# Turning the experts' rows on VectorE: 32x32 squares that the loads bring to their partitions

## The chip, the cores and the metric

The kernel runs on one core of a Trainium2 chip. The metric is the device time of one execution in microseconds; a smaller one is better. Before the change it is 262.52 us, the median of three runs (262.42 to 263.04). TensorE multiplies matrices, VectorE (DVE in the profile), ScalarE (ACT) and GpSimd (POOL) work on elements, SyncE (SP) issues most of the transfers between HBM and the on-chip memory.

## The reference, cut to what matters

Two blocks follow each other. The first is a state-space scan over chunks (Mamba2): for 4 sequences with 8 heads of 768 steps it gives rows of 32 numbers. The heads of a step are put side by side, so that there are 3072 tokens of 256 numbers. The second block sends each token to one of 8 experts:

```python
x = attn_out.transpose(0, 2, 1, 3).reshape(B * S, H * D)      # 3072 x 256
logits = x @ w_gate                                            # 3072 x 8
expert_idx = np.argmax(logits, axis=1)
probs = softmax(logits)                                        # + 1e-09 in the sum
gate_w = probs[np.arange(N), expert_idx]
for e in range(8):
    xe = x[expert_idx == e]
    h = np.maximum(xe @ w1[e], 0.0)                            # 256 -> 1024
    out[expert_idx == e] = gate_w[...] * (h @ w2[e])           # 1024 -> 256
```

Everything is in fp32.

## The kernel before, in words

**Scan and routing, up to about 70 us.** Twelve steps (`d` from 0 to 11) compute the scan for 256 tokens each. `rows(d)` turns a step's result on TensorE into one row per token, and its constant matrix `turn` appends the terms of the logits; `rows_out(d)` multiplies by a decay on VectorE and stores the row in the tile `rt`. A row has 320 words in two halves of 160 (128 words of the token, then 32 terms of the logits), and one word more for the token's number (`TOK`), 321 words or 1284 bytes. `logits_of`, `choose`, `rank` and `ranked` find each token's expert and its place there. `place(k)` has GpSimd scatter 128 rows to the tensor `x_hbm` in HBM, which has a stretch of rows for each expert. `cut` and the extra place rules see to it that the first 256 rows of experts 0 and 1 are there before the last groups are placed. `empty_rest` writes empty rows behind each expert's last token.

**Experts, from about 70 us on.** There are 16 jobs: pass 0 takes the first 256 places of each expert (`P1`), pass 1 up to 192 further ones (`P2`), two experts at a time, where the two half tiles of 64 rows share one tile of 128 partitions (`xh`). For a job `m_load(i)` brings the rows from `x_hbm` with the token on the partitions, by DMAs on SyncE's queue. For a matmul the token's words have to be on the partitions. `m_xT(i, pp)` does that: TensorE transposes each tile of 128x128 (L519) into a PSUM bank, VectorE copies it to `xT` (L521, L525, L527), and `gates` computes the softmax weight from the row's terms of the logits: on VectorE a sum (L358), a maximum and a difference, on ScalarE an exponential (L492), on VectorE a sum and a reciprocal. `m_h(i)` computes the first layer in 8 slices `f` (L557), each followed by a relu on ScalarE into `hT` (L566); `m_y(i)` the second layer (L592), whose result is scaled by the gate (L577, L579) and scattered by GpSimd to the output under the token's number (L570).

What sets the order: the engines' streams are written out by hand (`tc.manual_schedule()`), and each engine runs its own in that order. In pass 0 `m_xT(i + 1)` stands inside `m_h(i)`, between slices 4 and 5, and so does the exponential in ScalarE's stream. For i = 1 the checks of `over()` stand there too, ahead of it. In pass 1 `m_xT(i + 2)` stands between the first layers of a pair and their second layers. The DMA queue of SyncE is served in its order: after job 1's load the load of job 2, the 8 pieces of expert 2's weights, the load of job 3, and so on. A load of `x_hbm` waits for the scatters that stand before it in the program, and a scatter to `x_hbm` waits for the loads that stand before it. Job 0 has a version of its own (`m_xT0`), whose result ScalarE copies (L507).

Of the kernel before, what the change touches and what calls it, by code (L numbers as in the profile page):

```python
# [46 lines left out]
def ssd_then_moe(ctx, tc, xs_in, ae_in, wgx, w_gate, w1, w2, gx, gb, gc, ga, out):  # L47
# [416 lines left out]
    def m_load(i):  # L464
        p, e = jobs[i]
        if p == 0:
            xs = mo.tile([128, 2, W], FP32, name="xs", bufs=7)
            nc.sync.dma_start(out=xs, in_=x_hbm[e * NR:e * NR + P1, :].rearrange("(t p) w -> p t w", p=128))
            ex[i]["xs"] = [xs[:, t] for t in range(2)]
            ex[i]["all"] = xs  # L470
            return
        xs = mo.tile([128, 2, W], FP32, name="xs", bufs=7)
        nc.sync.dma_start(out=xs[:, 0], in_=x_hbm[e * NR + P1:e * NR + P1 + 128, :])
        ex[i]["xs"] = [xs[:, 0]]
        ex[i]["all"] = xs
        if e % 2 == 0:
            xh = mo.tile([128, W], FP32, name="xh", bufs=2)
            for u in range(2):
                r0 = (e + u) * NR + P1 + 128
                nc.sync.dma_start(out=xh[64 * u:64 * u + 64, :], in_=x_hbm[r0:r0 + 64, :])  # L480
            ex[i]["xh"] = ex[i + 1]["xh"] = xh

    def gates(rows, n):
# [3 lines left out]
        logits(l, rows)  # L487
# [12 lines left out]
    def m_xT0():  # L500

        ex[0]["xT"] = mo.tile([128, KT, P1], FP32, name="xT", bufs=4)
        for k in range(KT):
            q = h_next()[:, 0:P1]
            for t, xs in enumerate(ex[0]["xs"]):
                nc.tensor.transpose(q[:, 128 * t:128 * t + 128], xs[:, 160 * k:160 * k + 128], ident)
            nc.scalar.copy(ex[0]["xT"][:, k], q)  # L507

    def m_xT(i, pp):
        p, e = jobs[i]  # L510
        for u in range(1 + p):
            ex[i + u]["xT"] = mo.tile([128, KT, P1], FP32, name="xT", bufs=4)
        tiles = [xs for u in range(1 + p) for xs in ex[i + u]["xs"]] + ([ex[i]["xh"]] if p else [])
        q = []
        for t, xs in enumerate(tiles):
            if t % 2 == 0:
                q.append(h_next().rearrange("p (t k m) -> p t k m", t=2, k=KT))
            for k in range(KT):
                nc.tensor.transpose(q[-1][:, t % 2, k], xs[:, 160 * k:160 * k + 128], ident)  # L519
        if p == 0:  # L520
            nc.vector.tensor_copy(ex[i]["xT"].rearrange("p k (t m) -> p t k m", t=2), q[0])  # L521
            ex[i]["g"] = gates(ex[i]["all"], 2)
            return
        for u in range(2):
            nc.vector.tensor_copy(ex[i + u]["xT"][:, :, 0:128], q[0][:, u])  # L525
# [455 lines left out]
```

## Time and profile before

| | before |
|---|---|
| median of 3 runs | 262.52 us (262.42 to 263.04) |
| the profiled execution | 261.87 us |
| its span in the trace | 260.2 us |
| TensorE busy | 246.1 us (95%) |
| VectorE, ScalarE, GpSimd busy | 88.5, 88.3, 84.3 us |
| granted TensorE clock, mean over the span | 0.989 |
| DMA | 39.29 MB, mean 151 GB/s |

The times of the profile come from one execution; 1.67 us of it lie outside the span. An engine's busy time is the sum over its instructions; neighbouring matmuls overlap, so what one of them costs in the stream is read from the starts of it and of the next, not from its duration. The granted clock is the share of TensorE's full clock that the chip allowed. The share of DMA is the mean over 16 DMA engines; where packets overlap it can pass 1. The word behind an arrow in a row is what ended the wait ahead of the instruction.

### The profile page before, as it was taken

How to read it: one execution, taken by the hardware profiler on the slowest of the kernel's cores; microseconds unless marked ns; L12 is line 12 of the kernel's file. 1: busy time of each engine (PE TensorE's matmuls, PEld its weight loads, DVE VectorE, ACT ScalarE, POOL GpSimd, SP SyncE). 2: the span in 40 equal slices, each digit the busy share in tenths (PEclk: the TensorE clock that was granted, in tenths of full speed). 3: DMA queues.
4: the chain of work that ended last, by engine and by line, in shares of the span. 5: the costliest groups of instructions: out<-in, count | busy, mean ns of one | idle time of the engine just before them, and what ended most of it. 6: DMA issues, size and time to landing. Idle time of an engine off the chain costs nothing. (4 is left out here: it accounts for less than half of the span.)

```text
span 260.2 us, 5524 instructions
## 1 busy us (share of the span) xinstructions
PE 246.1 (95%) x2072; PEld 207.8 (80%) x2072; DVE 88.5 (34%) x286; ACT 88.3 (34%) x291; POOL 84.3 (32%) x149
## 2 busy tenths in 40 slices
PE   8898899979699999999999999999999999999992
PEld 5576677656588888888888888888998968989781
DVE  5899687667522130202020201106125015052000
ACT  4575557530141323232231313232250520623300
POOL 3645768862635133341331111110311111113031
PEclk9999999997999999999999999999999999999998
DMA  6999878326323996967969601010103101201001
GB/s 195 309 370 332 290 228 289 142 78 207 135 78 91 337 403 207 334 215 256 279 221 319 212 25 45 0 40 4 44 5 83 37 4 44 73 5 39 3 15 43
DMA packets 21049, 39.29 MB, mean 151 GB/s; under 512 B 3004, under 2 KB 8446, under 8 KB 20992
## 3 DMA queue, kind: packets, MB, share of 16 engines
q1 hardware_dynamic: 18000, 30.12, 35.3%
q0 software_dynamic: 2880, 8.41, 8.7%
q8 instruction: 29, 0.48, 0.8%
q14 instruction: 28, 0.23, 0.3%
q10 hardware_dynamic: 112, 0.05, 0.1%
HBM read 29.51 MB, written 9.59 MB: 150 GB/s over the span
## 5 line engine op out<-in xcount | busy, mean ns | idle before, releaser
L557 PE MATMUL h_ps<-xT,w 128*128 128x256 f32 (+3 forms) x512 | 90.7, 334 | 0.3 <-ACT xT L507 0.2
L557 PEld LDWEIGHTS h_ps<-xT,w 128*128 128x128 f32 x512 | 80.2, 190 | 7.3 <-ACT xT L507 0.5
L592 PE MATMUL y_ps<-w,hT 128*128 128x256 f32 x384 | 85.2, 380 | 0.2 <-ACT hT L566 0.2
L592 PEld LDWEIGHTS y_ps<-w,hT 128*128 128x128 f32 x384 | 72.5, 190 | 10.6 <-ACT hT L566 0.6
L570 POOL DMA_INDIRECT out_dram<-yo,xs x24 | 23.8, 990 | 94.1 <-ACT yo L579 55.1
L277 DVE TENSOR_TENSOR M<-g,mask 128x1024 f32<-128x1024 f32 x24 | 28.2, 1216 | 8.4 <-PE g L272 5.7
L566 ACT ACTIVATE hT<-h_ps 128x256 f32<-128x256 f32 x64 | 23.3, 381 | 20.7 <-PE h_ps L557 15.9
L408 POOL DMA_INDIRECT x_hbm<-rows,pos x24 | 23.8, 993 | 15.1 <-DVE less L426 5.9
L521 DVE COPY xT<-h_ps 128x512 f32<-128x512 f32 x7 | 4.8, 692 | 64.1 <-PE h_ps L519 34.8
L632 ACT ACTIVATE hT<-h_ps 128x128 f32<-128x128 f32 (+2 forms) x64 | 18.3, 292 | 24.1 <-PE h_ps L557 23.3
L342 PEld LDWEIGHTS r<-turn,yT 128*128 128x128 f32 x96 | 14.0, 197 | 8.2 <-issue 4.3
L579 ACT ACTIVATE yo<-y_ps,t_gt 128x256 f32<-128x256 f32 x14 | 6.6, 474 | 40.5 <-PE y_ps L592 40.5
L342 PE MATMUL r<-turn,yT 128*128 128x160 f32 x96 | 16.9, 320 | 3.7 <-issue 3.0
L329 PE MATMUL y<-M,xp 128*32 128x128 f32 x384 | 15.1, 277 | 3.6 <-DVE M L277 2.7
L335 ACT COPY yT<-y 128x512 f32<-128x512 f32 (+1 forms) x13 | 7.1, 554 | 29.4 <-PE y L329 17.9
L525 DVE COPY xT<-h_ps 128x256 f32<-128x256 f32 x8 | 3.0, 419 | 39.1 <-PE h_ps L519 39.1
L265 POOL TENSOR_TENSOR xp<-xs_n,Ei 128x256 f32<-128x256 f32 x23 | 13.8, 620 | 5.5 <-DVE last L240 3.3
L329 PEld LDWEIGHTS y<-M,xp 128*32 128x32 f32 x384 | 10.3, 109 | 6.6 <-issue 4.3
L260 ACT ACTIVATE cm<-xs_n,par 128x128 f32<-128x128 f32 x46 | 15.1, 419 | 1.2 <-DMA xs_n<-in_xs_dram 1.2
L492 ACT ACTIVATE t_sub<-t_sub 128x8 f32<-128x8 f32 (+1 forms) x20 | 4.2, 211 | 32.9 <-DVE t_sub L491 31.4
L272 PE MATMUL g<-cm,xs_n 32*128 32x256 f32 x192 | 15.1, 431 | 0.0
L570 POOL DMA_INDIRECT out_dram<-yh,xh x4 | 3.9, 984 | 34.2 <-ACT yh L606 21.9
(126 smaller groups left out, 167.0 us busy)
## 6 DMA issues: line engine op xcount, KB each, us to landing
w<-in_w_dram SPq DMA_DIRECT2D x64, 256.0 KB
xs_n<-in_xs_dram SPq DMA_DIRECT2D x20, 320.0 KB
xs<-x_hbm SPq DMA_DIRECT2D x8, 321.0 KB
xs<-x_hbm SPq DMA_DIRECT2D x8, 160.5 KB
xs_n<-in_xs_dram SPq DMA_DIRECT2D x4, 192.0 KB
x_hbm<-zrows SPq DMA_DIRECT2D x1, 642.0 KB
xh<-x_hbm SPq DMA_DIRECT2D x8, 80.2 KB
xs_n<-in_xs_dram SPq DMA_DIRECT2D x4, 128.0 KB
```

The lines of the kernel that those rows point to most:

```text
L260: nc.scalar.mul(t[:, u], st[n]["CT"], par[:, u:u + 1])
L265: eng.tensor_tensor(out=t, in0=st[n]["x"].rearrange("p (h d) -> p h d", d=D), in1=bc(Ei[:, n, :, None], [128, NH, D]), op=ALU.mult)
L272: nc.tensor.matmul(g_ps[:, q, n % 2], lhsT=st[n]["BT"][r], rhs=st[n]["cm"][r].rearrange("p u i -> p (u i)"), start=True, stop=True)
L277: nc.vector.tensor_tensor(out=t, in0=g_ps[:, :, n % 2].rearrange("p q (u i) -> p q u i", u=2), in1=bc(mask[:, None, None, :], [128, 4, 2, ...
L329: nc.tensor.matmul(y_ps[o:o + D, h // 4, CH * s:CH * s + CH], lhsT=st[n]["xp"][:, D * h:D * h + D], rhs=st[n]["M"][:, h], start=first, sto ...
L342: nc.tensor.matmul(r_ps[:, s, 160 * t:160 * t + 160], lhsT=sd[d]["yT"][:, t, CH * s:CH * s + CH], rhs=turn[:, t].rearrange("p e h -> p (e ...
L408: s_ = nc.gpsimd.indirect_dma_start(out=x_hbm[:, :], out_offset=bass.IndirectOffsetOnAxis(ap=at, axis=0), in_=row, in_offset=None)
L557: nc.tensor.matmul(p[:, 0:n], lhsT=w[:, c:c + 128], rhs=xT[:, t, 0:n], start=(t == 0), stop=(t == KT - 1))
L566: nc.scalar.activation(ex[i]["hT"][:, f, 0:n], q, func=ACT.Relu)
L570: return nc.gpsimd.indirect_dma_start(out=out[:, :], out_offset=bass.IndirectOffsetOnAxis(ap=tok, axis=0), in_=yo[:, :], in_offset=None, b ...
L592: nc.tensor.matmul(p, lhsT=ex[i]["hT"][:, f, 128 * t:128 * t + 128], rhs=w_sb[e][1][:, f * DM:f * DM + DM], start=(f == 0), stop=(f == FT ...
L632: nc.scalar.activation(ex[i + u]["hT"][:, f, 0:n], q, func=ACT.Relu)
```

## The change

The rows in HBM get another order: the 256 words of the token first, in one piece, then the 64 terms of the logits, then the token's number sixteen times, 336 words or 1344 bytes. `rows_out` writes the two parts with one multiply each, for both halves of the step. For jobs 1 to 15 `m_load` no longer brings whole rows. Four DMAs bring the words: the c-th takes words 64c to 64c + 63 of each row, a piece of 256 bytes, to partitions 32c to 32c + 31, where row number r in a group of 32 decides the partition. A fifth DMA brings the rest of the rows (logit terms and number, 320 bytes), with the token on the partitions, into a small tile `lt`, and for pass 1 two more bring it for the half tiles (`lh`). `m_xT` then has one VectorE instruction per job, which turns all squares of 32 by 32: after it the words are on the partitions. The order of words on the partitions is another one than before, and the weights are laid out for it before the launch (`by_d`). Job 0 is still turned by TensorE. The transposes and PSUM banks of the other jobs go.

```diff
-            nc.gpsimd.tensor_copy(rt[g][:, :, TOK].bitcast(I32), tok_i[:, R0[g]:R0[g] + n])
+            nc.gpsimd.tensor_copy(rt[g][:, :, TOK:W].bitcast(I32), bc(tok_i[:, R0[g]:R0[g] + n, None], [128, n, W - TOK]))
...
     def rows(d):
-            nc.tensor.matmul(r_ps[:, s, 160 * t:160 * t + 160], lhsT=sd[d]["yT"][:, t, CH * s:CH * s + CH],
+            nc.tensor.matmul(r_ps[:, s, 256 * t:256 * t + 160], lhsT=sd[d]["yT"][:, t, CH * s:CH * s + CH],
...
     def rows_out(d):
-        for s in range(2):
+        for a, b, o in ((0, D, 0), (D, DE, DM)):
             nc.vector.tensor_tensor(
-                out=rt[g][:, k + s, 0:RW].rearrange("p (t e h) -> p t e h", t=KT, h=4),
-                in0=r_ps[:, s, 0:RW].rearrange("p (t e h) -> p t e h", t=KT, h=4),
-                in1=bc(Er[:, n + s].rearrange("p (t h) -> p t h", h=4)[:, :, None, :], [128, KT, DE, 4]), op=ALU.mult)
+                out=rt[g][:, k:k + 2, o:o + KT * 4 * (b - a)].rearrange("p s (t e h) -> p s t e h", t=KT, h=4),
+                in0=r_ps.rearrange("p s (t z) -> p s t z", t=KT)[:, :, :, 4 * a:4 * b].rearrange(
+                    "p s t (e h) -> p s t e h", h=4),
+                in1=bc(Er[:, n:n + 2].rearrange("p s (t h) -> p s t h", h=4)[:, :, :, None, :],
+                       [128, 2, KT, b - a, 4]), op=ALU.mult)
...
     def m_load(i):
-        if p == 0:
-            xs = mo.tile([128, 2, W], FP32, name="xs", bufs=7)
+        if i == 0:
+            xs = mo.tile([128, 2, W], FP32, name="xs")
...
+        r0, n = e * NR + P1 * p, (P1, P2)[p]
+        xb = mo.tile([128, P1 // 32 * 64], FP32, name="xb", bufs=4)
+        for c in range(4):
+            nc.sync.dma_start(out=xb[32 * c:32 * c + 32, 0:2 * n].rearrange("p (r z) -> p r z", z=64),
+                              in_=x_hbm[r0:r0 + n, 64 * c:64 * c + 64].rearrange("(r j) z -> j r z", j=32))
+        ex[i]["xb"] = xb[:, 0:2 * n].rearrange("p (r i k) -> p k r i", k=KT, i=32)
+        lt = mo.tile([128, 2, MID], FP32, name="lt", bufs=7)[:, 0:2 - p]
+        nc.sync.dma_start(out=lt, in_=x_hbm[r0:r0 + 128 * (2 - p), DM:W].rearrange("(t p) w -> p t w", p=128))
...
-    def m_xT(i, pp):
+    def m_xT(i):
...
-            for k in range(KT):
-                nc.tensor.transpose(q[-1][:, t % 2, k], xs[:, 160 * k:160 * k + 128], ident)
-        if p == 0:
-            nc.vector.tensor_copy(ex[i]["xT"].rearrange("p k (t m) -> p t k m", t=2), q[0])
...
+        for j in range(i, i + 1 + p):
+            ex[j]["xT"] = mo.tile([128, KT, P1], FP32, name="xT", bufs=4)
+            nc.vector.transpose(ex[j]["xT"][:, :, 0:n].rearrange("p k (r j) -> p k r j", j=32), ex[j]["xb"])
+        for j in range(i, i + 1 + p):
+            ex[j]["g"] = gates(ex[j]["lt"], 2 - p)
```

On TensorE, around the fifth slice of job 1's first layer (L557) and the start of its second layer (L592); L434 and L435 belong to the checks of `over()`, and `w_1` are expert 1's weights. Before:

```order
L434 LDWEIGHTS ones_bf
L434 MATMUL r<-cnt,ones_bf 128x8
L435 LDWEIGHTS ones_bf
L435 MATMUL r<-weak,ones_bf 128x1
L519 MATMUL h_ps_1211<-ident,xs 128x128 x4
L557 MATMUL h_ps_1212<-xT,w_1_87 128x256 x2
```

and now, where L438 and L439 are the same checks:

```order
L438 LDWEIGHTS ones_bf
L438 MATMUL r<-cnt,ones_bf 128x8
L439 LDWEIGHTS ones_bf
L439 MATMUL r<-weak,ones_bf 128x1
L557 MATMUL h_ps_1210<-xT,w_1_87 128x256 x2
```

The four transposes of job 2 are gone from between the slices.

On SyncE, from the rest of expert 1's weights over the loads of jobs 1 and 2 to the weights of expert 2 (`w_2`) and the load of job 3. Before:

```order
L203 DMA w_1_88<-in_w_dram 128x512 x4
L468 DMA xs<-x_hbm 128x2x321 x2
L203 DMA w_2_89<-in_w_dram 128x512 x4
L203 DMA w_2_90<-in_w_dram 128x512 x4
L468 DMA xs<-x_hbm 128x2x321
```

and now (`xb` are the words, `lt` the rest of the rows):

```order
L204 DMA w_1_88<-in_w_dram 128x512 x4
L481 DMA xb<-x_hbm 32x8x64 x4
L485 DMA lt<-x_hbm 128x2x80
L481 DMA xb<-x_hbm 32x8x64 x4
L485 DMA lt<-x_hbm 128x2x80
L204 DMA w_2_89<-in_w_dram 128x512 x4
L204 DMA w_2_90<-in_w_dram 128x512 x4
L481 DMA xb<-x_hbm 32x8x64 x4
L485 DMA lt<-x_hbm 128x2x80
```

Each load has become five DMAs at the same place in the queue.

## Rows read from the trace of the kernel before

**Rows 1.** The page, busy time, share of the span and instructions by engine.
```profile
PE 246.1 (95%) x2072; PEld 207.8 (80%) x2072; DVE 88.5 (34%) x286; ACT 88.3 (34%) x291; POOL 84.3 (32%) x149
```

**Rows 2.** Busy time by stage; stretch, length, each engine, clock, DMA share, GB/s.
```profile
core 0: us, PE busy (x) PEld busy (x) DVE busy (x) ACT busy (x) POOL busy (x), PEclk, DMA share, GB/s
85.20:170.76 85.56, 85.56 (x412) 75.31 (x410) 12.18 (x58) 23.98 (x66) 20.21 (x28) 1.00 0.63 216
170.76:260.20 89.44, 84.15 (x537) 74.14 (x535) 20.40 (x98) 25.54 (x89) 14.79 (x15) 0.99 0.10 30
```

**Rows 3.** TensorE's waits for the second layer: total us, times, longest.
```profile
PE y_ps L592 <- ACT hT L566: 0.2, 1, 0.2
```

**Rows 4.** Timeline of TensorE, pass 0: start, length, instructions merged.
```profile
103.81 0.60 PE L519 MATMUL h_ps<-ident,xs 128*128 128x128 f32 x4
104.25 2.76 PE L557 MATMUL h_ps<-xT,w 128*128 128x256 f32 x12
```

**Rows 5.** Line L519 on TensorE: durations in ns (min/median/max), first and last start.
```profile
L519 PE MATMUL h_ps<-ident,xs x44: 272/273/330, 77.8 to 228.1; 128*128 128x128 f32 x44
L519 PE MATMUL h_ps<-ident,xh x8: 272/273/273, 175.5 to 228.3; 128*128 128x128 f32 x8
```

**Rows 6.** Timeline of TensorE, end of pass 0 (job 7).
```profile
175.07 0.60 PE L519 MATMUL h_ps<-ident,xs 128*128 128x128 f32 x4
...
175.73 2.76 PE L557 MATMUL h_ps<-xT,w 128*128 128x256 f32 x12
178.32 2.32 PE L592 MATMUL y_ps<-w,hT 128*128 128x256 f32 x10
180.83 5.02 PE L592 MATMUL y_ps<-w,hT 128*128 128x256 f32 x22 [0.18 <-ACT hT L566]
```

**Rows 7.** Timelines of VectorE, ScalarE and TensorE around job 2's turn.
```profile
91.59 0.14 DVE L456 TENSOR_SCALAR nk<-f_any 1x1 int32<-1x1 f32 x1
91.67 0.69 DVE L521 COPY xT<-h_ps 128x512 f32<-128x512 f32 x1
92.28 0.28 DVE L358 TENSOR_REDUCE t_l<-xs 128x16 f32<-128x128 f32 x1
...
93.06 0.21 ACT L492 ACTIVATE t_sub<-t_sub 128x16 f32<-128x16 f32 x1 [3.01 <-DVE t_sub L491]
93.19 0.92 ACT L566 ACTIVATE hT<-h_ps 128x256 f32<-128x256 f32 x3
...
92.59 7.07 PE L592 MATMUL y_ps<-w,hT 128*128 128x256 f32 x32
```

**Rows 8.** Timelines of SyncE's queue and GpSimd: loads of jobs 1, 2, last scatters.
```profile
72.28 0.38 SPq L468 DMA_DIRECT2D xs<-x_hbm  x1
...
82.69 0.38 SPq L468 DMA_DIRECT2D xs<-x_hbm  x1
...
76.02 0.99 POOL L408 DMA_INDIRECT x_hbm<-rows,pos  x1 [4.09 <-DMA xs<-x_hbm]
```

**Rows 9.** ScalarE's DMA queue: packets, MB, share of 16 engines over the span.
```profile
q10 hardware_dynamic: 112, 0.05, 0.1%
```

**Rows 10.** Busy time by stretch, columns as in rows 2: job 1's load; weights.
```profile
73.00:75.00 2.00, 2.00 (x11) 1.75 (x10) 0.35 (x3) 0.79 (x3) 0.00 (x0) 1.00 0.59 164
94.00:98.00 4.00, 4.00 (x21) 3.51 (x20) 0.00 (x0) 0.58 (x2) 2.54 (x4) 1.00 1.06 411
```

**Rows 11.** Timeline of ScalarE, end of pass 0 (job 7).
```profile
175.28 0.38 ACT L566 ACTIVATE hT<-h_ps 128x256 f32<-128x256 f32 x1 [0.48 <-PE h_ps L557]
177.49 0.21 ACT L492 ACTIVATE t_sub<-t_sub 128x8 f32<-128x8 f32 x1 [1.83 <-DVE t_sub L491]
...
180.29 0.21 ACT L492 ACTIVATE t_sub<-t_sub 128x8 f32<-128x8 f32 x1 [1.20 <-DVE t_sub L491]
```

**Rows 12.** VectorE by form: count, busy us, mean ns, idle before.
```profile
L277 DVE TENSOR_TENSOR M<-g,mask 128x1024 f32<-128x1024 f32 x24 | 28.2, 1216 | 8.4 <-PE g L272 5.7 <-PE r L342 2.4
L351 DVE TENSOR_TENSOR rows<-r,Er 128x320 f32<-128x320 f32 x24 | 10.5, 480 | 3.2 <-issue 2.3 <-PE y L321 0.9
```

More of the change, by code (lines that the diff above doesn't have):

```diff
@@ L34 @@
 RW = NH * DE
+W = RW + 16
 TOK = RW
-W = RW + 1
+MID = W - DM
 P1, P2 = 256, 192
@@ L362, in logits_of @@
         g = grp[n]
-        logits(l_all[:, n:n + 2], rt[g][:, n - R0[g]:n - R0[g] + 2])
+        logits(l_all[:, n:n + 2], rt[g][:, n - R0[g]:n - R0[g] + 2, DM:W])
     def choose(g):
@@ L465, in m_load, with gates @@
         p, e = jobs[i]
-        if p == 0:
-            xs = mo.tile([128, 2, W], FP32, name="xs", bufs=7)
+        if i == 0:
+            xs = mo.tile([128, 2, W], FP32, name="xs")
             nc.sync.dma_start(out=xs, in_=x_hbm[e * NR:e * NR + P1, :].rearrange("(t p) w -> p t w", p=128))
-            ex[i]["xs"] = [xs[:, t] for t in range(2)]
-            ex[i]["all"] = xs
+            ex[i]["xs"] = xs
+            ex[i]["lt"] = xs[:, :, DM:W]
             return
[L472 to L477, printed above, removed]
+        r0, n = e * NR + P1 * p, (P1, P2)[p]
[6 more added lines that the diff above has]
+        nc.sync.dma_start(out=lt, in_=x_hbm[r0:r0 + 128 * (2 - p), DM:W].rearrange("(t p) w -> p t w", p=128))
+        ex[i]["lt"] = lt
+        if p and e % 2 == 0:
+            lh = mo.tile([128, 1, MID], FP32, name="lh", bufs=3)
             for u in range(2):
[L479 to L483, printed above, removed]
+                q = r0 + u * NR + 128
+                nc.sync.dma_start(out=lh[64 * u:64 * u + 64, 0], in_=x_hbm[q:q + 64, DM:W])
+            ex[i]["lh"] = ex[i + 1]["lh"] = lh
+    def gates(mid, n):
         sh = [128, n, E]
         l = mo.tile([128, 2, E], FP32, name="t_l", bufs=2)[:, 0:n]
-        logits(l, rows)
+        logits(l, mid)
         mx = mo.tile([128, 2], FP32, name="t_mx", bufs=2)[:, 0:n]
@@ L504, in m_xT0 @@
             q = h_next()[:, 0:P1]
-            for t, xs in enumerate(ex[0]["xs"]):
-                nc.tensor.transpose(q[:, 128 * t:128 * t + 128], xs[:, 160 * k:160 * k + 128], ident)
+            for t in range(2):
+                xs = ex[0]["xs"][:, t, 0:DM].rearrange("p (i k) -> p i k", k=KT)
+                nc.tensor.transpose(q[:, 128 * t:128 * t + 128], xs[:, :, k], ident)
             nc.scalar.copy(ex[0]["xT"][:, k], q)
-    def m_xT(i, pp):
+    def m_xT(i):
         p, e = jobs[i]
[L511 to L517, printed above, removed]
-            for k in range(KT):
-                nc.tensor.transpose(q[-1][:, t % 2, k], xs[:, 160 * k:160 * k + 128], ident)
-        if p == 0:
-            nc.vector.tensor_copy(ex[i]["xT"].rearrange("p k (t m) -> p t k m", t=2), q[0])
[L522 to L525, printed above, removed]
-        for u in range(2):
-            nc.vector.tensor_copy(ex[i + u]["xT"][:, :, 128:P2], q[1][:, 0, :, 64 * u:64 * u + 64])
-        for u in range(2):
-            ex[i + u]["g"] = gates(ex[i + u]["all"][:, 0:1], 1)
-        ex[i]["gh"] = gates(ex[i]["xh"][:, None, :], 1)
+        n = (P1, P2)[p]
+        for j in range(i, i + 1 + p):
[3 more added lines that the diff above has]
+            ex[j]["g"] = gates(ex[j]["lt"], 2 - p)
+        if p:
+            ex[i]["gh"] = gates(ex[i]["lh"], 1)
     H, Y, turn_no = [], [], [0, 0]
@@ L588, in m_y @@
         e = jobs[i][1]
-        for t, xs in enumerate(ex[i]["xs"]):
+        for t in range(2 - jobs[i][0]):
             p = y_next()
@@ L679, in general @@
                 for t in range(KT):
-                    nc.sync.dma_start(out=yT[:, t],
-                                      in_=y_hbm[ds(m * DM + 128 * t, 128), :].rearrange("(h d) t -> d h t", h=4))
+                    v = y_hbm[ds(m * DM + 128 * t, 128), :].rearrange("(a k d) s -> k d a s", a=2, k=KT)
+                    for k in range(KT):
+                        nc.sync.dma_start(out=yT[64 * t:64 * t + 64, k], in_=v[k])
                 p = y_next()
@@ L864, in ssd_then_moe @@
         count(LAST)
-        ex[0]["g"] = gates(ex[0]["all"], 2)
+        ex[0]["g"] = gates(ex[0]["lt"], 2)
         for i in range(E):
@@ L896, in between @@
                                                skip_runtime_bounds_check_because="a truth value"))
-                m_xT(i + 1, pp)
+                m_xT(i + 1)
             m_h(i, pp, between)
             if i == 0:
-                m_xT(1, pp)
+                m_xT(1)
             if i < E - 1:
@@ L912, in ssd_then_moe @@
                         m_load(i + u)
-                m_xT(i + 2, pp)
+                m_xT(i + 2)
             m_y(i, pp)
@@ L943, in by_d @@
     def by_d(v):
[L944 to L945 removed]
+        s = v.shape
+        v = v.reshape(*s[:-2], KT, 4, D, s[-1]).swapaxes(-3, -2).reshape(*s[:-2], 128, KT, s[-1])
+        return v.swapaxes(-3, -2)
     lay = {
```

26 lines of the change are left out of this document (12 added, 14 removed).

## The prediction

> **What bounds the kernel now.** I read the totals of the page first, then the busy time by stage, then who waited for whom, and last the timelines of two places where another engine comes close to stopping TensorE. TensorE is busy for 95% of the span [rows 1]. From 85 to 171 us, the first pass of the experts, it is busy without a gap, with VectorE busy 14% and ScalarE 28% of the time, and the second pass is alike up to its last 5 us [rows 2]; for a relu of ScalarE it waited once for a result of another engine, for 0.2 us [rows 3]. So what TensorE does there sets the end, at a granted clock of 1.00 (the 2.4 GHz level), and an instruction taken out of its stream shortens the run by the time to the start of the next one, as long as nobody else becomes late.
>
> **What goes from TensorE.** m_xT turned an expert's rows with 52 transposes, 44 of full tiles and 8 of the shared half tiles [rows 5]: four for each of experts 1 to 7, six for each of the four pairs of the second pass. Their own durations (273 ns) overlap, so I take starts: the four begin at 103.81 and the matmul behind them at 104.25, 0.44 us; the six take from 175.07 to 175.73, 0.66 us [rows 4, 6]. That is 7 x 0.44 + 4 x 0.66 = 5.72 us. The Trainium skill ("VectorE: DVE Perf Modes", The three transpose paths) gives a 128x128 TensorE transpose 390 ns; by it 52 would be worth 20.3 us. Here four pass in 0.44 us, so the trace decides and that figure is not used.
>
> The transposes of pair 0 had a second effect. In the last expert of pass 1 ScalarE needs three exponentials of the gates between its fifth and sixth relu. They waited for VectorE, which could begin only when TensorE had transposed: relu at 175.28, exponentials from 177.49, the last at 180.29 [rows 11]. TensorE did ten matmuls of the second layer (two for each of five slices), then stood until 180.83; twelve matmuls take 175.73 to 178.32, 0.216 us each, so ten end at 178.32 + 2.16 = 180.48 and it lost 0.35 us [rows 6]. Afterwards VectorE turns this pair as soon as its rows are loaded, long before. The first exponential can follow the fifth relu at 175.7, the third then comes 2.8 us later at 178.5, and the relu it holds up ends near 178.9, before TensorE asks at 177.66 + 2.16 = 179.8. Gain 0.35 us, with 0 as the lower end.
>
> **What VectorE gets.** One 32x32-square transpose of 512 columns per expert takes the place of a copy of 512 columns (0.69 us) [rows 7], two of 384 take the place of four smaller copies. The trace has no such transpose; the nearest row is the copy at 0.69 us, the upper bound a 512-column transpose as dear as the 1024-column multiply, 1.22 us [rows 12]; the lower end is nothing. VectorE has that time. The one tight place is expert 2, whose transpose stands behind the checks of over() in VectorE's order, and whose exponential stands between two relus of expert 1. Checks end at 91.59 + 0.14 = 91.73 now, and 0.44 us earlier afterwards, since TensorE reaches them earlier by one group: 91.29. From the logits (92.28) to the end of the next relu (93.19 + a third of 0.92) it takes 1.22 us. The second layer starts at 92.59 now, 0.88 us earlier afterwards (two groups), and asks for that relu after ten matmuls: 91.71 + 2.16 = 93.87 [rows 7]. So the transpose may take 1.36 us before it costs anything. I cost it at nothing.
>
> **What the loads get: the open term.** Each expert's load was one DMA of 256 rows of 1284 B; now it is four DMAs of 256 pieces of 256 B each, and one of 256 rows of 320 B, 1280 pieces or 80 for each of 16 engines. The old load kept the engines busy 0.59 of 2 us, 1.18 us for 16 rows: 74 ns a row [rows 10]. Let a piece cost c; a load then takes 80c - 1.18 us longer. For expert 1 this is passed on: the last group's scatters on GpSimd wait for all five DMAs (issue 72.28, first scatter 76.02), three more scatters are queued behind the first, and the load of expert 2, which SyncE issues at 82.69, waits for them [rows 8]. Expert 2's load is itself longer by the same. It lands at 82.69 + 3.74 + 2(80c - 1.18) = 84.07 + 160c. It is in time until 93.87 - 1.22 = 92.65, so c may be 54 ns; each ns above costs 0.16 us.
>
> What is c? By bytes alone: 2 KB weight rows at 411 GB/s and a share of 1.06 cost 84 ns, so 256 B cost 11 ns, the lower end [rows 10]. The upper end is the row of 1284 B, 74 ns. Nearest in size are ScalarE's 96 rows of 512 B with 16 closing packets: 112 packets in 0.1% of 16 engines' 260.2 us, 37 ns each (19 to 56 by the rounding) [rows 9]. I take 37 ns: expert 2 lands at 90.0, 2.7 us early, and the loads cost nothing. SyncE's issue (0.38 us each, 1.9 us for five) lies within the 3.0 us of the pieces. The weights of expert 2 follow in the same queue, 1 MB in 2.6 us, by 92.6 against a need at 92.59 + 7.07 - 0.88 = 98.8. For the other experts a step lasts 85.56 / 6 = 14.26 us with a DMA share of 0.63 [rows 2]; the extra 1.8 us raises it to 0.76, at 74 ns to 0.96, still under the whole.
>
> The Trainium skill speaks against this ("DMA: Bandwidth & Descriptors", Specifications): below 512 B the DMA engine reads, modifies and writes. No run here shows it yet. If it doubled the 37 ns, a mechanism that the rows allow, c would be 74 ns and expert 2 would stop TensorE for 160 x 0.020 = 3.2 us.
>
> **What the routing stage gets.** Two multiplies of 320 columns at 480 ns become one of 512 and one of 128. From 320 and 1024 columns (480 and 1216 ns) a column costs 1.05 ns and an instruction 146 ns, so 681 + 279 = 960 ns, as now [rows 12]. The split is finer and reads more dimensions; 0.1 us more in each of 12 steps would cost at most 1.2 us, 0.1 us less would give at most as much. I take 0. Six small GpSimd copies grow to 64 columns (under 0.2 us each, behind which the next head scaling has over 2 us), the scattered rows grow by 60 B, and the first expert is still turned by TensorE: nothing.
>
> **Sum.** The profiled execution took 261.87 us, 1.67 us around its span of 260.2, and lies 0.65 us under the median. 261.87 - 5.72 - 0.35 = 255.8; for the median 262.52 - 6.07 = 256.4 us.
>
> **Rivals.**
> *Part of the gain is lost to the pieces* (54 to 97 ns). For it: 74 ns is the price of the nearest row of the same tensor, and expert 2 has only 2.7 us to spare. Against: that row is five times as long. At 74 ns TensorE waits 3.2 us near 93 us: 259.6 us. The rule on 512 B gives the same time.
> *Slower: the pieces starve the start of the experts.* The same chain, GpSimd's scatters behind expert 1's load and SyncE's load of expert 2 behind them, takes all of the 6.1 us and 0.8 more when a piece costs more than 54 + 6.9 / 0.16 = 97 ns. At 110 ns: 256.4 + 9.0 = 265.4 us. Against it: no row shows a packet at saturation above 84 ns. For it: no row shows 256 B pieces either, and several DMAs in a row could each pay a start that the single load paid once.
> *The routing stage grows.* The finer multiply adds 1.2 us before the experts begin: 257.6 us. The stage's row prices speak against it.
> *The transposes are slow on VectorE.* At three times the copy, 2.1 us, expert 2 would wait 0.7 us, and 257.1 us remain; the other experts have the whole second layer as cover.
>
> **How the numbers follow.** The forecast as worked out has 0.66, with its own range 255.6 to 257.3; lost part of the gain 0.17 (257.3 to 261.7); slower 0.08; a longer routing stage or slow transposes 0.09. A measurement of this kernel tells 0.3%, 0.8 us, from no change. Faster by more than that: 0.66 + 0.09 + most of 0.17 = 0.88; within 0.04; slower 0.08. The range for 8 in 10 goes from 255.2 (a routing stage shorter by 1.2 us) to 260.5 us, past the 74 ns case.
>
> **What would show it.** Right: the second layer follows the first with no wait; six steps of 14.26 - 0.44 us; no wait near 180; VectorE transposes at 0.7 us; expert 2's logits on VectorE right behind its transpose near 92. Wrong: TensorE stands near 93 us until a relu that waits for an exponential, expert 2's last load lands after 92.7, GpSimd's first scatter of the last group starts later than 78 us, or the second layer of a later expert waits for a transposed tile.

## The result, and the profile after

The changed kernel takes 257.86 us (median of 6 runs, 254.24 to 258.68), the kernel before in the same sessions 263.74 us (6 runs, 262.42 to 265.41): ratio 0.9699, 95% interval 0.9648 to 0.9751. Ratios and intervals here compare only runs within 1.5% of the same kernel's fastest, while medians take all runs: 0.9699 rests on three runs of the changed kernel, one of them of 254.24 us, and the ratio of `warm` below leaves out a run of 414.31 us. The medians differ by 5.88 us; the prediction had 6.07 us and 256.4 us, with a kernel before that took 1.22 us less than in these sessions. Two later comparisons of the same two kernels, on two different chips, gave 257.34 against 263.61 (0.976, 0.9707 to 0.9813) and 251.28 against 256.8 (0.9779, 0.9749 to 0.9808). So the gain is 5.5 to 6.3 us by the medians, 2.2 to 3.0% by the ratios. The two profiled executions alone differ by less: 261.87 - 257.61 = 4.26 us.

The page's busy line after, in a span of 255.9 us (before: [rows 1]):

```profile
PE 241.0 (94%) x2020; PEld 202.2 (79%) x2020; DVE 88.8 (35%) x278; ACT 88.9 (35%) x291; POOL 84.2 (33%) x149
```

TensorE has exactly 52 instructions fewer; VectorE, ScalarE and GpSimd are as busy as before within 0.6 us. Its timeline after (start, length, instructions merged, count; in brackets the idle time just before and what ended it):

```profile
85.95 4.48 PE L557 MATMUL h_ps<-xT,w 128*128 128x256 f32 x20
...
93.00 7.07 PE L592 MATMUL y_ps<-w,hT 128*128 128x256 f32 x32
...
168.97 7.07 PE L557 MATMUL h_ps<-xT,w 128*128 128x256 f32 x32
175.88 7.07 PE L592 MATMUL y_ps<-w,hT 128*128 128x256 f32 x32
182.78 7.31 PE L557 MATMUL h_ps<-xT,w 128*128 128x128 f32 x64
...
196.88 2.48 PE L557 MATMUL h_ps<-xT,w 128*128 128x164 f32 x16
199.54 6.95 PE L557 MATMUL h_ps<-xT,w 128*128 128x164 f32 x48 [0.18 <-ACT hT L632]
...
217.01 7.31 PE L557 MATMUL h_ps<-xT,w 128*128 128x128 f32 x64
...
243.75 7.17 PE L592 MATMUL y_ps<-w,hT 128*128 128x256 f32 x32
```

and before, the same places:

```profile
85.16 4.48 PE L557 MATMUL h_ps<-xT,w 128*128 128x256 f32 x20
...
170.76 4.48 PE L557 MATMUL h_ps<-xT,w 128*128 128x256 f32 x20
...
200.39 9.07 PE L557 MATMUL h_ps<-xT,w 128*128 128x164 f32 x64
...
220.59 7.31 PE L557 MATMUL h_ps<-xT,w 128*128 128x128 f32 x64
...
248.01 7.17 PE L592 MATMUL y_ps<-w,hT 128*128 128x256 f32 x32
```

The reader is to see three things. First layers, such as that at 168.97, are one piece of 32 matmuls where four transposes stood in them before [rows 4]. The second layer at 175.88 runs through, where TensorE stood until 180.83 before [rows 6]. And there is one new stop: at 196.88 TensorE enters the second pair, does 16 matmuls (its four PSUM banks), and goes on only when a relu of ScalarE has emptied one.

What VectorE does for expert 2, and ScalarE behind it (same columns; compare [rows 7]):

```profile
92.39 0.14 DVE L460 TENSOR_SCALAR nk<-f_any 1x1 int32<-1x1 f32 x1
92.57 0.71 DVE L526 STREAM_TRANSPOSE xT<-xb 128x512 f32<-128x512 f32 x1
93.21 0.24 DVE L362 TENSOR_REDUCE t_l<-lt 128x16 f32<-128x128 f32 x1
...
93.96 0.22 ACT L503 ACTIVATE t_sub<-t_sub 128x16 f32<-128x16 f32 x1 [3.10 <-DVE t_sub L502]
```

The transpose follows the checks of `over()` without a wait for a DMA, and the logits follow it: the load was in time, and the checks set the moment, as before.

The load of expert 1, now four loads of squares and one of the rest of the rows (SyncE's queue and GpSimd; compare [rows 8]), and the DMA engines meanwhile (columns as in [rows 2]; the last two are DMA share and GB/s):

```profile
73.74 1.81 SPq L481 DMA_DIRECT2D xb<-x_hbm  x4
75.60 0.45 SPq L485 DMA_DIRECT2D lt<-x_hbm  x1
86.50 1.79 SPq L481 DMA_DIRECT2D xb<-x_hbm  x4
...
80.04 0.98 POOL L412 DMA_INDIRECT x_hbm<-rows,pos  x1 [7.32 <-DVE t_sub L502]
```

```profile
74.00:75.00 1.00, 1.00 (x6) 0.87 (x6) 0.35 (x2) 0.09 (x2) 0.00 (x0) 1.00 0.17 27
75.00:76.00 1.00, 1.00 (x6) 0.90 (x5) 0.00 (x0) 0.52 (x2) 0.00 (x0) 1.00 0.70 116
76.00:77.00 1.00, 1.00 (x6) 0.87 (x5) 0.00 (x0) 0.52 (x2) 0.00 (x0) 1.00 0.71 137
77.00:78.00 1.00, 1.00 (x7) 0.87 (x6) 0.58 (x1) 0.42 (x2) 0.00 (x0) 1.00 0.37 73
```

The engines' share adds up to 0.17 + 0.70 + 0.71 + 0.37 = 1.95 us for 80 pieces each (64 of 256 bytes and 16 of 320): 24 ns a piece. From the first issue to the first scatter of the last group it is 80.04 - 73.74 = 6.30 us (3.74 before), and load 2 follows load 1 by 86.50 - 73.74 = 12.76 us (10.41 before).

### The profile page after: what moved, and what is told of

Its sections match the earlier page's. It is cut to its first block, busy times and chain, and to the rows that moved or that the text cites. A ratio compares the mean times of both kernels' runs of the same rounds, so it can differ in the third digit from the quotient of the medians.

```text
span 255.9 us, 5488 instructions
## 1 busy us (share of the span) xinstructions
PE 241.0 (94%) x2020; PEld 202.2 (79%) x2020; DVE 88.8 (35%) x278; ACT 88.9 (35%) x291; POOL 84.2 (33%) x149
## 5 line engine op out<-in xcount | busy, mean ns | idle before, releaser
L557 PE MATMUL h_ps<-xT,w 128*128 128x256 f32 (+3 forms) x512 | 90.5, 335 | 0.6 <-issue 0.4
L557 PEld LDWEIGHTS h_ps<-xT,w 128*128 128x128 f32 x512 | 80.6, 190 | 8.6 <-ACT hT L632 0.6
L592 PE MATMUL y_ps<-w,hT 128*128 128x256 f32 x384 | 85.0, 380 | 0.0
L592 PEld LDWEIGHTS y_ps<-w,hT 128*128 128x128 f32 x384 | 72.6, 190 | 10.5 <-issue 0.8
L570 POOL DMA_INDIRECT out_dram<-yo,lt x22 | 21.8, 989 | 58.1 <-DVE yo L577 31.1
L566 ACT ACTIVATE hT<-h_ps 128x256 f32<-128x256 f32 x64 | 24.1, 383 | 25.2 <-PE h_ps L557 17.4
L505 DVE TENSOR_REDUCE t_se<-t_sub 128x1 f32<-128x8 f32 (+1 forms) x20 | 3.3, 164 | 63.3 <-ACT t_sub L503 48.8
L526 DVE STREAM_TRANSPOSE xT<-xb 128x384 f32<-128x384 f32 (+1 forms) x15 | 9.2, 630 | 41.9 <-DMA xb<-x_hbm 38.7
L412 POOL DMA_INDIRECT x_hbm<-zrows,rest x8 | 7.7, 961 | 39.3 <-DMA lt<-x_hbm 23.7
L343 PE MATMUL r<-turn,yT 128*128 128x160 f32 x96 | 16.2, 312 | 3.6 <-issue 2.0
L343 PEld LDWEIGHTS r<-turn,yT 128*128 128x128 f32 x96 | 13.3, 189 | 8.0 <-issue 4.2
L266 POOL TENSOR_TENSOR xp<-xs_n,Ei 128x256 f32<-128x256 f32 x23 | 13.7, 618 | 6.7 <-DVE last L241 3.6
L570 POOL DMA_INDIRECT out_dram<-yh,lh x4 | 3.9, 983 | 33.5 <-ACT yh L606 21.5
```

The lines of the kernel that those rows point to most:

```text
L266: eng.tensor_tensor(out=t, in0=st[n]["x"].rearrange("p (h d) -> p h d", d=D), in1=bc(Ei[:, n, :, None], [128, NH, D]), op=ALU.mult)
L343: nc.tensor.matmul(r_ps[:, s, 256 * t:256 * t + 160], lhsT=sd[d]["yT"][:, t, CH * s:CH * s + CH], rhs=turn[:, t].rearrange("p e h -> p (e ...
L412: s_ = nc.gpsimd.indirect_dma_start(out=x_hbm[:, :], out_offset=bass.IndirectOffsetOnAxis(ap=at, axis=0), in_=row, in_offset=None)
L557: nc.tensor.matmul(p[:, 0:n], lhsT=w[:, c:c + 128], rhs=xT[:, t, 0:n], start=(t == 0), stop=(t == KT - 1))
L566: nc.scalar.activation(ex[i]["hT"][:, f, 0:n], q, func=ACT.Relu)
L570: return nc.gpsimd.indirect_dma_start(out=out[:, :], out_offset=bass.IndirectOffsetOnAxis(ap=tok, axis=0), in_=yo[:, :], in_offset=None, b ...
```

## The experiments

**The transposes alone, and their return.** `no_turn_before` is the kernel before without the 52 transposes (VectorE copies words that are not turned):

```
-                nc.tensor.transpose(q[-1][:, t % 2, k], xs[:, 160 * k:160 * k + 128], ident)
...
-            nc.vector.tensor_copy(ex[i]["xT"].rearrange("p k (t m) -> p t k m", t=2), q[0])
+            nc.vector.tensor_copy(ex[i]["xT"].rearrange("p k (t m) -> p t k m", t=2),
+                                  ex[i]["all"][:, :, 0:RW].rearrange("p t (k z) -> p t k z", k=KT)[:, :, :, 0:128])
...
```

> The kernel before, with the 52 TensorE transposes of experts 1 to 15 left out: VectorE copies the untransposed words from the loaded tiles instead of PSUM (the output is then not the reference's). Loads, rows and routing stage are those of before. Theory 1 (TensorE's program sets the end, and what the change adds costs next to nothing): 5.2 to 6.1 us faster than before (ratio 0.977 to 0.980), like the whole change; an expert's step from m_h to m_h falls from 14.27 to about 13.8 us. Theory 2 (the transposes were worth more, and the change gave a part back to loads, turns and rows): 7 us or more faster. Theory 3 (the gain of the change came from elsewhere, the rows or the loads): 3 us or less faster.

`after_pe_back` is the changed kernel with as many transposes at the old places:

```
+        for t in range(2 + p):
+            if t % 2 == 0:
+                q = h_next().rearrange("p (t k m) -> p t k m", t=2, k=KT)
+            for k in range(KT):
+                nc.tensor.transpose(q[:, t % 2, k], ident, ident)
```

> The changed kernel with 52 TensorE transposes of the identity put back at the old places; nothing reads them. Theory 1: they cost what they cost before, 7 x 0.44 + 4 x 0.66 = 5.7 us, less about 0.7 us where TensorE now waits for ScalarE between pairs and could do them in the wait: 4.9 to 5.7 us over the changed kernel, so ratio 0.985 to 0.998 against before by the changed kernel's fast runs (0.970), or 0.996 to 1.000 by the medians. Theory 2 (the changed kernel waits for loads and turns somewhere, and the transposes disappear in such waits): 3 us or less over the changed kernel, ratio below 0.985.

Measured by medians: 257.76 against 263.46 us before, 5.70 us faster (0.9897, 0.9724 to 1.007, a wide interval from 4 runs that does not exclude no gain); with the transposes back 263.69 us, 0.23 over before (1.0012, 0.9892 to 1.0132) and 6.35 over the 257.34 us of the changed kernel in the second comparison, on another chip. The intervals alone would not tell theories 1 and 2 apart, so the timelines decide. TensorE of `no_turn_before`:

```profile
85.31 4.48 PE L553 MATMUL h_ps<-xT,w 128*128 128x256 f32 x20
...
168.32 7.07 PE L553 MATMUL h_ps<-xT,w 128*128 128x256 f32 x32
...
196.41 9.54 PE L553 MATMUL h_ps<-xT,w 128*128 128x164 f32 x64
205.89 3.65 PE L600 MATMUL y_ps<-w,hT 128*36 128x256 f32 x32
...
243.18 7.17 PE L588 MATMUL y_ps<-w,hT 128*128 128x256 f32 x32
```

and of `after_pe_back`:

```profile
85.58 4.48 PE L562 MATMUL h_ps<-xT,w 128*128 128x256 f32 x20
...
171.18 4.48 PE L562 MATMUL h_ps<-xT,w 128*128 128x256 f32 x20
```

Without transposes six steps take 168.32 - 85.31 = 83.01 us, 13.84 each; with them 171.18 - 85.58 = 85.60, 14.27 each, as before (170.76 - 85.16 = 85.60). From the first layer of expert 1 to the last second layer it is 162.85 us before, 157.80 after and 157.87 (85.31 to 243.18) in `no_turn_before`. So removing the transposes alone gives the whole gain of this stretch, and nothing else of the change costs anything there. Theory 3 falls; theory 2 has no place left in this stretch. In `after_pe_back` the stretch lasts 163.95 us, 6.15 over the changed kernel and more than the 4.9 to 5.7 us expected: TensorE stops there for 1.41 us in the second layer of the third pair, a stop that the kernel before does not have and whose cause was not looked for.

**The rows in DRAM alone.** `layout_only` has the new rows and rows_out, with the old whole-row loads (six buffers instead of seven) and TensorE transposes of every second word:

```
...
+                v = xs[:, 0:DM].rearrange("p (i k) -> p i k", k=KT)[:, :, k]
+                nc.tensor.transpose(q[-1][:, t % 2, k], v, ident)
...
```

> The changed kernel's rows in DRAM (words of the two halves side by side, logits and 16 token words behind them), with whole-row loads and the TensorE transposes of before. Theory 1 (the routing stage is neutral): within 0.8 us of before, ratio 0.997 to 1.003, and m_h(0) starts at 70.4 give or take 0.8 us. Rival (the row writing costs the stage what the profile of the changed kernel showed): 0.9 us slower, ratio 1.0035, m_h(0) at 71.3 or later, with VectorE's row writes late at each step of the stage.

Measured: 263.34 against 263.46 us (1.0023, 0.9932 to 1.0114). The new multiplies of rows_out take what was worked out from [rows 12] (by form in the changed kernel: count, busy us, mean ns):

```profile
L352 DVE TENSOR_TENSOR rows<-r,Er 128x512 f32<-128x512 f32 x12 | 8.2, 681 | 1.8 <-PE r L343 1.6 <-PE y L322 0.2
...
L352 DVE TENSOR_TENSOR rows<-r,Er 128x128 f32<-128x128 f32 x12 | 3.3, 279 | 0.0
```

In its profile the first expert's first layer began at 71.07 us, 70.36 before and 71.28 after. But `no_turn_before`, whose routing stage is that of before, came to its first second layer at 78.40, and before reached the same place (its transposes in front) at 77.81. That is 0.59 us between two profiles with the same routing stage, so differences of this size between single profiles are spread; the medians say neutral, but only within about 1% or 2.5 us.

**Smaller pieces.** `half_pieces` is the changed kernel with eight loads of 128-byte pieces in place of four of 256:

```
...
+            for h in (0, 32):
+                nc.sync.dma_start(
+                    out=xb[32 * c:32 * c + 32, 0:2 * n].rearrange("p (r z) -> p r z", z=64)[:, :, h:h + 32],
+                    in_=x_hbm[r0:r0 + n, 64 * c + h:64 * c + h + 32].rearrange("(r j) z -> j r z", j=32))
```

> The changed kernel with pieces of 128 bytes instead of 256: eight square loads an expert instead of four. Theory 1 (a piece has a price of some 25 ns whatever its length, and the load of expert 2 is the one with little to spare): SyncE issues 4 x 0.45 = 1.8 us more a load, the load itself takes 2 us more, expert 1's squares come 2 to 4 us later without a stop, expert 2's Exp waits for its words so that the last relus of expert 1 come late, and TensorE stops in the second layer of expert 1: 2 to 6 us slower than the changed kernel, ratio to before 0.980 to 0.995. Rival (the loads are hidden whatever they cost, or the price goes with bytes): within 0.6 us of the changed kernel.

Measured: 272.01 against 263.46 us (1.0355, 0.9979 to 1.073), 14.7 us over the changed kernel's 257.34 us of the other session. The expectation was right in direction, wrong in size and in one premise. DMA share during expert 1's load (columns as above):

```profile
74.00:76.00 2.00, 2.00 (x15) 1.68 (x15) 0.82 (x6) 1.14 (x4) 0.00 (x0) 1.00 0.20 29
76.00:78.00 2.00, 2.00 (x11) 1.77 (x10) 0.00 (x0) 0.77 (x2) 0.00 (x0) 1.00 0.51 75
78.00:80.00 2.00, 2.00 (x11) 1.77 (x10) 0.00 (x0) 0.93 (x3) 0.00 (x0) 1.00 0.24 32
80.00:82.00 2.00, 2.00 (x11) 1.76 (x10) 1.14 (x3) 0.22 (x1) 0.00 (x0) 1.00 0.22 44
```

2 x (0.20 + 0.51 + 0.24 + 0.22) = 2.34 us for 144 pieces (128 of 128 bytes and 16 of 320), 16 ns each, where the changed kernel's 80 took 1.95 us. A piece of half the length is cheaper, so the price is not one per piece; nor does it quite go with the bytes, as the same bytes take 0.39 us more. That is little against 14.7 us. What grew more is the issuing: from the first issue to the end of the last it is 5.50 us (74.08 to 79.58) where it was 2.31. SyncE's queue of `half_pieces`, and then its waits (total us, times, longest):

```profile
74.08 5.01 SPq L482 DMA_DIRECT2D xb<-x_hbm  x8
...
115.81 3.85 SPq L482 DMA_DIRECT2D xb<-x_hbm  x8
...
131.78 4.63 SPq L482 DMA_DIRECT2D xb<-x_hbm  x8
```

```profile
SPq L482 <- DMA x_hbm<-zrows,rest: 26.8, 4, 7.7
```

and the worst stop of its TensorE:

```profile
190.50 7.01 PE L594 MATMUL y_ps<-w,hT 128*128 128x256 f32 x22 [4.98 <-ACT hT L568]
```

Load 4 goes out at 115.81, load 5 at 131.78: 16 us apart, where an expert takes 13.8. Each load waits for the empty rows that GpSimd wrote before it, and those wait for the load before (in the changed kernel's profile their wait ends with the load's last DMA, 23.7 us in 3 waits; in that of `half_pieces` the profile names the weights that follow this load in the queue). The loads fall behind a little with each expert, and TensorE stops: 0.6 us at expert 1, then 1.6, 0.5, 2.1 and 5.0 us at experts 4 to 7. The last stop costs more than itself: behind it the granted clock is 0.50 from 190 to 194 us, the 1.2 GHz level, and the 22 matmuls above take 7.01 us where 22 at full clock take 5.02 [rows 6], so that this second layer lasts 7.2 us longer than the 6.91 us of the others. The same two issues are 13.6 to 13.8 us apart in the changed kernel (109.18 and 122.73 in its first profile, 106.94 and 120.73 in the second comparison) and 10.8 in the kernel before (100.59 and 111.34). The changed kernel waits for empty rows just as long (27.4 us in 4 waits): the loop runs in every version, and what `half_pieces` changed is its period.

**The loop cut.** `half_regrouped` is `half_pieces` with one thing moved:

```
-                if 1 <= i <= 4:
-                    for e in range(2 * i - 2, 2 * i):
+                if i == 4:
+                    for e in range(E):
                         empty_rest(e)
```

> half_pieces with one thing moved: the eight writes of empty rows to the row table, two each in the steps of experts 1 to 4 before, all stand in the step of expert 4. Theory 1 (half_pieces lost its 14 us to a loop: a load waits for the empty rows written before it, these wait for the load before, and one turn of the loop took some 16 us where an expert takes 13.8): loads 4 to 6 follow one another without the wait, only one long wait of some 12 us is left before load 8, and 8 us or more of the 14 come back: ratio to before 0.985 to 1.005. Rival (the pieces themselves, their issues and their time in the queues, make the loads late): 4 us or less comes back, ratio above 1.015.

Measured: 257.21 against 256.8 us (1.0005, 0.9978 to 1.0032), so 0.4 us over before instead of 8.6, on another chip: 8 us came back, theory 1. The changed kernel on that chip takes 251.28 us, so 5.9 us are still lost. Its TensorE has one stop left in pass 0:

```profile
84.49 2.32 PE L594 MATMUL y_ps<-w,hT 128*128 128x256 f32 x10
91.62 7.92 PE L594 MATMUL y_ps<-w,hT 128*128 128x256 f32 x22 [4.81 <-ACT hT L568]
99.38 7.07 PE L559 MATMUL h_ps<-xT,w 128*128 128x256 f32 x32
```

From 99.38 on every step is 13.81 us. What is left is the place that the prediction named for starving, the load of expert 2: this second layer lasts 99.38 - 84.49 = 14.89 us instead of 6.91, 8.0 us more, of which some 5 are the stop and some 3 the matmuls behind it, at a granted clock of 0.50 from 91 to 97 us.

**The new stop at the pairs.** `gates_together` works out the three gates of a pair with one set of instructions:

```
...
-        for j in range(i, i + 1 + p):
-            ex[j]["g"] = gates(ex[j]["lt"], 2 - p)
-        if p:
-            ex[i]["gh"] = gates(ex[i]["lh"], 1)
+        g = gates([ex[i]["lt"], ex[i + 1]["lt"], ex[i]["lh"]], 3)
...
```

> The changed kernel with the three gates of a pair worked out in one set of instructions: one Exp of 128x24 on ScalarE instead of three of 128x8, 8 VectorE instructions instead of 18. Theory 1 (between pairs ScalarE's chain of three Exps, 1.4 us apart, is what TensorE now waits for at the second pair by 0.5 us and at the fourth by 0.2 us): TensorE starts the second layer of the pair without a stop, 0.5 to 0.8 us faster than the changed kernel. Rival (ScalarE's way into the next case of the switch sets it, whatever the Exps take): within 0.2 us of the changed kernel, the stop stays.

> The changed kernel once more, as the measure for the three others of this call. Both theories: ratio to before 0.970 to 0.980.

Measured: 257.54 us (0.9807, 0.9754 to 0.9861) beside 257.34 us of the changed kernel (0.976, 0.9707 to 0.9813): no gain that can be measured. The place itself did change. ScalarE of the changed kernel before the stop at 196.88:

```profile
193.09 0.21 ACT L503 ACTIVATE t_sub<-t_sub 128x8 f32<-128x8 f32 x1 [2.38 <-issue]
...
195.90 0.21 ACT L503 ACTIVATE t_sub<-t_sub 128x8 f32<-128x8 f32 x1 [1.21 <-DVE t_sub L502]
199.18 0.91 ACT L632 ACTIVATE hT<-h_ps 128x164 f32<-128x164 f32 x4 [3.08 <-issue]
```

and TensorE of `gates_together` at the same pair:

```profile
196.96 9.16 PE L562 MATMUL h_ps<-xT,w 128*128 128x164 f32 x64
```

Two exponentials and 2.8 us less on ScalarE, and the first layer of that pair runs through: 9.09 us to the next group, at 206.05. Over all profiles it takes 9.01 to 9.10 us with the gates together (4 profiles) and 9.10 to 9.54 with them apart and the transposes gone (7). But TensorE entered that pair 0.3 us later here (7.21 us from 189.75 to 196.96, against 6.95 from 189.93 to 196.88), so that of the 0.45 us by which the way from this pair to the third became shorter little is left in the sum; why it entered later was not found. The rival is refuted for the stop, and right for the time.

**TensorE's clock at the end of the routing stage.** In the profiles before and after, the granted clock falls to half (the 1.2 GHz level) between 60 and 64 us, behind a wait of TensorE for VectorE (in the profile after 2.50 us, up to 60.17). `keep_clock` and `both` (the latter with the gates together) give it small products to do in that wait:

```
+            if d == 10:
+                for _ in range(24):
+                    nc.tensor.matmul(r_ps[:, 0, 416:512], lhsT=none_bf[:, 0:128], rhs=none_bf[:, 0:96], start=True,
+                                     stop=True, skip_group_check=True)
```

> The changed kernel with 24 small bf16 products into unused columns of PSUM, in TensorE's wait for VectorE in the last chunk step but one (57.7 to 60.2 us). Theory 1 (TensorE's granted clock of 0.5 from 60.2 to 63.6 us follows its idle time before): the granted clock stays at 1.0 there, and the routing stage ends 0.8 to 1.8 us earlier than in the changed kernel. Rival (the fall has another cause, or the path there is VectorE's and the pool's): the same time within 0.3 us, or up to 1 us slower where the products run past the wait.

> The changed kernel with both edits of this call: the gates of a pair together and the products in TensorE's wait. If the gains stand apart, the sum of the two: 1.3 to 2.6 us faster than the changed kernel; if neither holds, within 0.3 us of it.

Measured: 257.08 us (0.9788, 0.9737 to 0.9838) and 257.07 us (0.9776, 0.9732 to 0.982), like the changed kernel's 257.34. The stretch 60 to 64 us in the profile of `keep_clock`, and then of `both` (clock third from the end):

```profile
60.00:64.00 4.00, 3.77 (x67) 3.14 (x67) 3.18 (x8) 0.58 (x1) 1.12 (x4) 1.00 0.55 177
```

```profile
60.00:64.00 4.00, 4.00 (x59) 2.74 (x58) 1.84 (x8) 0.59 (x1) 0.77 (x3) 0.62 0.52 164
```

The same products, with gaps of at most 0.52 us between them in both profiles, and once the clock held (expert 1 begins 2.2 us earlier than in the changed kernel's profile), once it fell. `warm` (with the gates together) used 8 and 6 products of float32 words at two places:

```
...
+            nc.tensor.matmul(r_ps[:, 0, 416:512], lhsT=ident, rhs=ident[:, 0:96], start=True, stop=True,
+                             skip_group_check=True)
...
```

> gates_together with products of float32 words into unused columns of PSUM at two places where TensorE waits at the end of the routing stage: 8 of 128x96 before the second pair of weighings in the last chunk step but one, and 6 before the last rows are turned. Theory 1 (TensorE's granted clock of 0.5 in 60 to 64 us, and in some profiles in 70 to 73 us, follows these two waits): the granted clock stays at 1.0 from 56 to 74 us and the kernel is 1 to 2.5 us faster than the changed kernel, ratio to before 0.966 to 0.972. Rival (the fall has another cause): clock and time as in the changed kernel within 0.5 us.

> The changed kernel once more, as the measure for the run of this call that keeps TensorE at work. Both theories: ratio to before 0.972 to 0.980, m_y(0) at 79.1 us give or take 0.6.

252.25 us (0.9802, 0.9766 to 0.9837) beside 251.28 us: no gain, and no test, since on that chip the changed kernel's clock had not fallen either. What makes it fall, and whether it can be held, stays open.

**What that last comparison showed.** The changed kernel there came to its first second layer at 71.07 us, where 79.1 was expected, began expert 1 some 8 us earlier than in the first profile, and stopped:

```profile
85.02 2.32 PE L592 MATMUL y_ps<-w,hT 128*128 128x256 f32 x10
88.92 5.02 PE L592 MATMUL y_ps<-w,hT 128*128 128x256 f32 x22 [1.58 <-ACT hT L566]
```

VectorE and ScalarE at that time:

```profile
87.00 0.71 DVE L526 STREAM_TRANSPOSE xT<-xb 128x512 f32<-128x512 f32 x1 [2.44 <-DMA xb<-x_hbm]
...
88.38 0.22 ACT L503 ACTIVATE t_sub<-t_sub 128x16 f32<-128x16 f32 x1 [5.51 <-DVE t_sub L502]
88.50 0.91 ACT L566 ACTIVATE hT<-h_ps 128x256 f32<-128x256 f32 x3
```

Here VectorE waits for expert 2's squares, the exponential behind it, three relus of expert 1 behind that, and TensorE behind them. The second layer takes 93.78 - 85.02 = 8.76 us instead of 6.91, so 1.85 us are lost. Load 1 went out at 71.28, 13.7 us before this layer; in the first profile at 73.74, 19.3 us before it. So the spare time of expert 2's load was what TensorE lost in the routing stage. `warm` fits this: on the same chip it began expert 1 at 80.02 instead of 77.97 us, and its second layer of expert 1 ran through. Before has no profile on this chip; whether it stops there too is not known.

`late_gates` takes the relus out from behind that exponential, with the gates together as well:

```
...
-                m_xT(i + 1)
             m_h(i, pp, between)
-            if i == 0:
-                m_xT(1)
+            m_xT(i + 1)
```

> The changed kernel with two edits: the turn and the gates of expert i+1 stand behind the last relu of expert i's first layer instead of in its middle (they hold no TensorE work any more), and the three gates of a pair are worked out in one set of instructions, as in gates_together. Theory 1 (where the routing stage ends early, the changed kernel stops 1.6 us in the second layer of expert 1, because the last relus stand behind an Exp that waits for the load of expert 2; and ScalarE's three Exps cost 0.3 to 0.5 us at the pairs): no such stop in any step, experts' steps of 13.81 us throughout, ratio to before 0.965 to 0.972 on a chip where the changed kernel has 0.978, and 0.2 to 0.5 us under the changed kernel where it had no stop. Rival (the load of expert 2 comes too late for the first layer of expert 2 as well, so that the wait only moves from the middle to the end of the step): the same time as the changed kernel within 0.3 us.

Measured: 256.94 against 263.36 us (0.9744, 0.9692 to 0.9797), on a chip where the routing stage ended late (m_h(1) at 86.02) and no stop was to be removed. The relus now stand ahead of the exponential (91.54, 92.40 and 93.27 us, the exponential at 94.03). Whether this saves the 1.85 us where they are lost was not seen, and no version was shown to beat the changed kernel.

## Why the prediction was right

*The sum.* The mechanism is right; that the medians come within 0.2 us of 6.07 is in part luck. In the profiled pair 4.3 us of the span are gained, 1.8 less than forecast. From the first layer of expert 1 to the last second layer it is 5.05 us, where 5.72 - 0.44 + 0.35 = 5.63 was forecast (the first four transposes stand ahead of that stretch); the other 1.2 us are missing before it.

*TensorE's 5.72 us.* Right, and shown both ways. In the trace six steps take 168.97 - 85.95 = 83.02 us instead of 85.60: 2.58 where 6 x 0.44 = 2.64 was forecast. The 390 ns that the prediction quotes from the Trainium skill ("VectorE: DVE Perf Modes", The three transpose paths) and sets aside stand there for bf16. The ones taken out here are of fp32, at 273 ns each [rows 5] and 0.11 us from one start to the next.

*The stop of the last expert in pass 0.* Right: from its first layer to the first pair 182.78 - 168.97 = 13.81 us, 14.92 before; 1.11 gained where 0.66 + 0.35 = 1.01 was forecast, and the second layer has no stop.

*The pairs.* Here the step failed that let an instruction taken out of TensorE's stream count in full "as long as nobody else becomes late" and then priced nobody at the pairs. From the second pair to the third it is 217.01 - 196.88 = 20.13 us, 20.20 before: 0.07 of 0.66 arrived. ScalarE's way from one pair to the next (out of the switch, three exponentials, into the next case) had just been covered by the six transposes. `no_turn_before`, with none of the other edits, has it too (9.48 us for that first layer, 9.00 in the kernel before), so it is the price of a shorter TensorE stream and not of the new loads. About 0.6 us, all that this stretch of the trace has under the forecast.

*VectorE's transposes.* Right: 712 ns for 512 columns and 559 ns for 384, against 0.69 us for the copy, well within the 1.36 us of room.

*The loads.* The outcome was right in the profiled run, the sizes were not. The piece was put at 37 ns and measured 24 ns, and 16 ns with most pieces halved. By the bytes of the weight rows it would have been 11 ns [rows 10], so a small piece does cost about twice what its bytes would. The rival with 74 ns is not seen. For 1000 bytes an engine takes 41 ns in the weight rows of 2 KB, 58 in the old rows of 1284 bytes [rows 10], 91 in the new pieces and 109 in the halved ones: the price rises with every shortening. The rule of the Trainium skill on transfers under 512 B ("DMA: Bandwidth & Descriptors", Specifications) did not double the 37 ns, as the prediction had asked; whether it has a part in the 24 ns, these four prices cannot tell. The issuing, put under the cover of the pieces, lasts 75.60 + 0.45 - 73.74 = 2.31 us and is longer than their 1.95. The first scatter of the last group came at 80.04 us, behind the 78 us that the prediction had named as a sign of being wrong: its load went out 1.46 us later than before, and it followed 2.56 us later on that, not 1.8. In the second and third comparison it followed 1.4 and 1.3 us later (72.19 to 77.33 and 71.28 to 76.30). Nothing came of it in the first profile, because the checks of `over()` held expert 2's transpose longer. So the chain that the rival called starving exists: `half_regrouped` shows its price when the issues double, and `half_pieces` that of a second loop, over the empty rows, which the prediction did not name. In the changed kernel itself the chain cost something in one profile only, where the routing stage ended early: 1.85 us.

*The routing stage.* The multiplies were right: 681 + 279 = 960 ns as worked out. That the stage as a whole gets nothing is not settled. In the profile after TensorE came to expert 1 at 85.95 us, where 85.16 - 0.44 = 84.72 was forecast. The four other profiles with the changed rows and loads in which the clock fell in this stage (`after_again`, `gates_together`, `both`, `late_gates`) have 85.77 to 86.09; `no_turn_before`, with the old rows and without transposes, has 85.31. So the change may cost some 0.5 to 0.8 us there, and the interval of `layout_only` (0.9932 to 1.0114) neither shows nor excludes it.

## What to carry to other kernels

When instructions leave the engine that sets the end, go through the other engines' chains from one group to the next and ask which of them the removed instructions had covered; a chain that just fitted becomes the new stop. Count DMA issues as well as bytes: a queue's issue time, passed on through loads and stores that wait for each other on one tensor, makes a loop, and such a loop is free until its period passes that of the step. And margins read from one profile hold for that run: here a routing stage that ended earlier uncovered the wait that the first profile had hidden.

## What the runs showed of the hardware

A 32x32-square transpose of float32 on VectorE costs 712 ns for 128x512 and 559 ns for 128x384. One load kept the 16 DMA engines busy for 1.95 us in 80 pieces of 256 and 320 bytes for each engine, and the same bytes for 2.34 us in 144 pieces of 128 and 320 bytes. SyncE issued one such load in about 0.45 us when nothing held it, and eight in a row in 3.7 to 7.5 us. In the profile after, ScalarE stood 2.4 us behind the last instruction of a case of a switch (2.35 to 2.38 in three places) and once 3.1 us ahead of the first of the next, with nothing that the profile shows to wait for. The granted clock of TensorE fell to half for some 3.5 us in the routing stage in ten of fourteen profiles, in nine of them behind a wait of 1.8 to 2.6 us, in `both` with no gap over 0.52 us. It fell again behind the two stops of some 5 us in the experts (0.50 from 190 to 194 us in `half_pieces`, from 91 to 97 us in `half_regrouped`), and not behind a stop of 1.6 us (1.00 from 140 to 145 us in `half_pieces`).
